# The second MoE's first layer as seven block products per unit, with the tokens in two rounds

## The chip, the core and the metric

The kernel runs on one core of a Trainium2 chip. The metric is the device time of one execution in microseconds. Five engines matter: TensorE (PE; its weight loads are listed apart, as PEld), VectorE (DVE), ScalarE (ACT), GpSimd (POOL) and SyncE (SP), which issues all transfers here. TensorE adds up its sums in PSUM, eight banks of 512 float32 per partition; the other memory is SBUF.

## What is computed

An attention with packed queries, then two MoE layers on 2304 tokens of 512 features. The change is in the last one.

```python
def _moe_ref(x, w_in, w_out):                  # first MoE: 512 -> 2048 -> 512
    h = np.maximum(x @ w_in, 0.0)
    return (h * h @ w_out)

def _moe2_ref(x, w_gate, w1, w2):              # second MoE: 8 experts, 512 -> 1024 -> 512
    P = np.exp(logits - logits.max())          # logits = x @ w_gate
    for _ in range(8):                         # the balance
        P /= P.sum(1, keepdims=True) + 1e-09
        P /= P.sum(0, keepdims=True) + 1e-09
        P *= N / E
    for e in range(E):
        h = np.maximum(x @ w1[e], 0.0)
        out += P[:, e:e + 1] * (h @ w2[e])     # every expert on every token
```

## The kernel before

Values are kept to float32 precision by splitting: a number is the sum of a rounded high half and the rest, both of the type float32r, and a product is three matmuls: high x high, high x low, low x high (a loop over `(x, y)` in `(0, 0), (0, 1), (1, 0)`). ScalarE writes the high half, VectorE (for activations) or GpSimd (for weights) subtracts it for the low half.

The stages follow one another: attention of four batches, the first MoE (`g_unit`, `h1_unit` and `x2_unit`; chunks of 288 tokens, result transposed in `X2`), the gate (`logits`, `gate_exp`, then eight steps of `rows_step` and `cols_step`), the second MoE. A scheduler sets the order of each engine's instructions from the order in which they are written; all queues run in order.

In the second MoE the 8 x 1024 hidden features are 16 groups `g` of 512, each of four columns `m` of 128. The tokens are five chunks, four of 512 and one of 256. `split_x` has split the whole of `X2` into `XS` before. `h2_mm` (L512) forms the hidden features of a chunk and one `m`: four blocks of 128 input features x three matmuls into one bank, 12 matmuls. `h2_evac` reads it out: ScalarE writes the high half with its ReLU (L520), VectorE the low half (L521). `y_unit` (L536) forms 128 tokens of the output: four `m` x three matmuls, 12 again, with the hidden features stationary and w2 moving. VectorE adds it, times the gate's column, to `acc` in SBUF (L549; L546 for the first expert, whose factors come late). A group's weights are loaded once, 2 x 2 transfers of 512 KB (L90), and are split by `split_w` (L120 on ScalarE, L121 on GpSimd) during the group before.

Four PSUM banks serve `h2_mm` and four `y_unit`. `logits` is a split product as well, with the gate's weights padded to 128 columns (L460), and is turned round by 18 transposes (L465); the balance takes its column sums with a float32 matmul of all ones (`cols_mm`, L492).

## Time and profile before

| | us |
|---|---|
| median of three runs | 2027.56 (2023.48 to 2029.18) |
| the profiled execution, its own time | 2027.71 |
| its span, first to last instruction | 2025.9 |
| TensorE busy | 1998.5 |
| VectorE / ScalarE / GpSimd busy | 771.9 / 502.5 / 261.5 |
| first layer of the second MoE on TensorE (L512) | 804.4 |
| second layer (L536) | 798.4 |
| first MoE on TensorE (L332, L313) | 234.7, 128.5 |

Busy times of matmuls count from start to a modelled end, and neighbours overlap; what a matmul costs is read from the distance of the work that they release.

### The profile page before, as it was taken

How to read it: one execution, taken by the hardware profiler on the slowest of the kernel's cores; microseconds unless marked ns; L12 is line 12 of the kernel's file. 1: busy time of each engine (PE TensorE's matmuls, PEld its weight loads, DVE VectorE, ACT ScalarE, POOL GpSimd, SP SyncE). 2: the span in 40 equal slices, each digit the busy share in tenths (PEclk: the TensorE clock that was granted, in tenths of full speed). 3: DMA queues.
4: the chain of work that ended last, by engine and by line, in shares of the span. 5: the costliest groups of instructions: out<-in, count | busy, mean ns of one | idle time of the engine just before them, and what ended most of it. 6: DMA issues, size and time to landing. Idle time of an engine off the chain costs nothing.

```text
span 2025.9 us, 24381 instructions
## 1 busy us (share of the span) xinstructions
PE 1998.5 (99%) x10250; PEld 1719.0 (85%) x10250; DVE 771.9 (38%) x1376; ACT 502.5 (25%) x987; POOL 261.5 (13%) x209
## 2 busy tenths in 40 slices
PE   8999999999999999999999999999999999999999
PEld 6898999998888888888888888888888888888887
DVE  5979887654222222222222222222222222222222
ACT  3646454532323121202021211111112121111110
POOL 2313321210202020202020202010101010110100
PEclk8999999999999999999999999999999999999999
DMA  7402210100001010101010101010000000000011
GB/s 254 157 22 75 72 43 22 43 22 1 32 11 43 1 42 0 42 1 42 1 42 0 42 1 42 1 42 11 32 11 32 11 32 11 31 14 29 1 42 52
DMA packets 21549, 71.04 MB, mean 35 GB/s; under 512 B 2368, under 2 KB 2368, under 8 KB 21440
## 3 DMA queue, kind: packets, MB, share of 16 engines
q1 hardware_dynamic: 21440, 69.49, 10.0%
q8 instruction: 80, 1.31, 0.3%
...
## 4 chain that ended last, share of the span: by engine, by line
PE 91%; DVE 7%; issue 1%; ACT 1%; POOL 0%; DVEq 0%; POOLq 0%; ACTq 0%
PE psh L512 39%; PE psy L536 39%; PE psy L332 7%; PE psh L313 3%; PE pp L200 1%; DVE cc L101 1%; DVE h L322 1%; DVE cm L105 1%; DVE g L300 1%; DVE s L320 1%; DVE cx L107 1%; PE psh L290 1%; PE s L168 0%; DVE x L339 0%; PE s L230 0%
## 5 line engine op out<-in xcount | busy, mean ns | idle before, releaser
L512 PE MATMUL psh<-x,w 128*128 128x512 f32 (+1 forms) x3840 | 804.4, 368 | 0.0
L536 PE MATMUL psy<-w,hh 128*128 128x512 f32 x3456 | 798.4, 389 | 0.0
L512 PEld LDWEIGHTS psh<-x,w 128*128 128x128 f32 x3840 | 670.4, 188 | 121.0
L536 PEld LDWEIGHTS psy<-w,hh 128*128 128x128 f32 x3456 | 647.4, 188 | 133.6
L520 ACT ACTIVATE hh<-psh 128x512 fp32r<-128x512 f32 (+1 forms) x320 | 177.6, 555 | 1203.0 <-PE psh L512 1202.9
L521 DVE SCALAR_TENSOR_TENSOR hh<-psh,hh 128x512 fp32r<-128x512 f32 (+1 forms) x320 | 204.0, 637 | 611.7 <-ACT hh L520 611.7
L549 DVE SCALAR_TENSOR_TENSOR acc<-psy,P,acc 128x512 f32<-128x512 f32 x252 | 189.1, 751 | 464.5 <-PE psy L536 464.5
L121 POOL TENSOR_TENSOR w<-raw,w 128x512 fp32r<-128x512 f32 x128 | 165.5, 1309 | 1424.4 <-ACT w L120 1413.0
L332 PE MATMUL psy<-h,w 128*128 128x288 f32 x1536 | 234.7, 297 | 7.6 <-DVE h L322 4.6
L332 PEld LDWEIGHTS psy<-h,w 128*128 128x128 f32 x1536 | 213.6, 188 | 12.4 <-DVE h L322 7.0
L313 PE MATMUL psh<-at,g 128*128 128x288 f32 x768 | 128.5, 296 | 2.3 <-DVE s L320 2.3
L313 PEld LDWEIGHTS psh<-at,g 128*128 128x128 f32 x768 | 111.0, 188 | 4.1 <-DVE s L320 3.2
L120 ACT ACTIVATE w<-raw 128x512 fp32r<-128x512 f32 x128 | 79.5, 626 | 43.3 <-PE psy L536 37.0
L321 ACT ACTIVATE h<-s 128x288 fp32r<-128x288 f32 x128 | 56.6, 443 | 74.5 <-DVE s L320 68.8
L322 DVE TENSOR_TENSOR h<-s,h 128x288 fp32r<-128x288 f32 x128 | 69.8, 549 | 8.5 <-ACT h L321 6.9
L320 DVE SCALAR_TENSOR_TENSOR s<-psh,r 128x288 f32<-128x288 f32 x128 | 57.4, 450 | 31.8 <-ACT r L317 31.2
L121 POOL TENSOR_TENSOR w<-cx,w 128x512 fp32r<-128x512 f32 x32 | 45.0, 1407 | 161.3 <-ACT w L120 125.9
L317 ACT ACTIVATE r<-psh 128x288 f32<-128x288 f32 x128 | 51.4, 404 | 49.3 <-PE psh L313 48.6
L103 POOL TENSOR_TENSOR cc<-cc,cr 128x512 int32<-128x512 int32 x32 | 45.3, 1417 | 46.7 <-DVE cc L101 30.1
L339 DVE TENSOR_TENSOR x<-psy,x 128x288 f32<-128x288 f32 x96 | 42.8, 451 | 20.9 <-PE psy L332 20.7
L300 DVE TENSOR_TENSOR g<-psh,g 64x512 fp32r<-64x512 f32 x64 | 43.6, 686 | 5.6 <-ACT g L299 4.4
L299 ACT ACTIVATE g<-psh 64x512 fp32r<-64x512 f32 x64 | 37.4, 591 | 11.0 <-PE psh L290 6.7
...
## 6 DMA issues: line engine op xcount, KB each, us to landing
raw<-w SPq DMA_DIRECT2D x64, 512.0 KB, 3.4
raw<-win SPq DMA_DIRECT2D x16, 512.0 KB, 3.8
raw<-wout SPq DMA_DIRECT2D x16, 512.0 KB, 3.8
...
```

The source lines that it names most:

```text
L120: nc.scalar.activation(w[:, 0, :], t, AF.Copy)
L121: nc.gpsimd.tensor_tensor(w[:, 1, :], t, w[:, 0, :].bitcast(F32), op=ALU.subtract)
L300: nc.vector.tensor_tensor(lo, ps[r:r + 64, :], hi.bitcast(F32), op=ALU.subtract)
L313: nc.tensor.matmul(ps, gw[:, x, m * 128:(m + 1) * 128], at[:, y, g, o:o + CT], start=(i == 0), stop=(i == 5))
L320: nc.vector.scalar_tensor_tensor(s, ps, 0.0, r, op0=ALU.max, op1=ALU.mult)
L322: nc.vector.tensor_tensor(h[:, 1, :], s, h[:, 0, :].bitcast(F32), op=ALU.subtract)
L332: nc.tensor.matmul(ps, w[:, x, d * 128:(d + 1) * 128], h[:, y, :], start=(i == 0), stop=(i == 11))
L512: nc.tensor.matmul(ps[:, :n], w[:, x, kd * 128:(kd + 1) * 128], XS[c][:, y, kd, :], start=(i == 0), stop=(i == 11))
L520: nc.scalar.activation(h[:, 0, :n], ps[:, :n], AF.Relu)
L521: nc.vector.scalar_tensor_tensor(h[:, 1, :n], ps[:, :n], 0.0, h[:, 0, :n].bitcast(F32), op0=ALU.max, op1=ALU.subtract)
L536: nc.tensor.matmul(ps, h[:, x, t * 128:(t + 1) * 128], w[:, y, :], start=(i == 0), stop=(i == 11))
L549: nc.vector.scalar_tensor_tensor(a, ps, P[:, tt, e:e + 1], a, op0=ALU.mult, op1=ALU.add)
```

## The change

The first layer of the second MoE is computed by the Strassen scheme with seven products. For a half-group of 256 hidden features the weights (512 inputs x 256 outputs) are four blocks of 256 inputs x 128 outputs: `A11`, `A12` belong to the first 128 outputs, `A21`, `A22` to the second. A group of tokens is cut into two halves, and its inputs are four blocks `B11`, `B12`, `B21`, `B22` (first index: inputs, second: half of the tokens). With S1 = A21 + A22, S2 = S1 - A11, S3 = A11 - A21, S4 = A12 - S2 and T1 = B12 - B11, T2 = B22 - T1, T3 = B22 - B12, T4 = B21 - T2, the four blocks of the result come out of A11 B11, A12 B21, S1 T1, S2 T2, S3 T3, S4 B22 and A22 T4. Each product is 2 x 3 matmuls, 42 a unit where 48 stood.

`unit` writes this out with three banks. X takes A11 B11, then S2 T2, S3 T3 and A22 T4 are added on top of what stands in it; between them X is copied to `s12` by ScalarE, and added to `s5` by VectorE. Y takes A12 B21, Z takes S1 T1 and S4 B22. Three additions on VectorE (L634, L645, L648) and three copies on ScalarE (L632, L639, L641) a unit are new, two of the additions in PSUM.

- Tokens: three groups `GROUPS` of 768, 512 and 1024, so products have 384, 256 and 512 columns. Round one runs groups 0 and 1 through the 32 half-groups of weights, round two runs group 2 through them in reverse; the half-group at the turn serves both. So weights are loaded 63 times a half-group, 126 transfers of 512 KB.
- `w1_blocks` forms S1 to S4 with four GpSimd operations of 256 columns per half-group; the splits of w1 are then four (the last of half width) instead of two for the same weights.
- `split_x` and `x_sums` split seven blocks per token group (B11, B21, B22, T1 to T4) at the start of group and round.
- `y_unit` sums two `m` instead of four: six matmuls (L596) and one accumulation on VectorE (L614), 576 of them instead of 288. They have two banks (`ybank`) instead of four; X, Y and Z of two units have six.
- `logits` is now 72 float32 matmuls (L513) with the tokens stationary and the gate's 8 columns moving; the transposes go. `X2` is held by token groups, so the additions of two chunks of the first MoE are in two pieces.

```diff
+NQ = 2 * NG
 NT = T // 128
-CHUNKS = [(c * 512, min(512, T - c * 512)) for c in range(-(-T // 512))]
+GROUPS = [(0, 384), (768, 256), (1280, 512)]
+ROUNDS = ((0, 1), (2,))
...
-    for g in range(NG):
-        for nm, src in (("w1", w1), ("w2", w2)):
-            for i in (0, 2):
-                splits += [((nm, g, i), len(loads), 0), ((nm, g, i + 1), len(loads), 1)]
-                loads.append(("f32", src[g, :, i:i + 2, :]))
+    seq2 = list(range(NQ)) + list(range(NQ - 2, -1, -1))
+    for n, g in enumerate(seq2):
+        for nm, src, parts in (("w1", w1, 4), ("w2", w2, 2)):
+            splits += [((nm, n, i), len(loads), i) for i in range(parts)]
+            loads.append(("f32", src[g // 2, :, 2 * (g % 2):2 * (g % 2) + 2, :].rearrange("p m n -> p (m n)")))
...
+    def w1_blocks(r, i):
+        a11, a12, a21, a22 = (r[:, j * 256:(j + 1) * 256] for j in range(4))
+        if i == 0:
+            t = wpools[2].tile([128, 1024], F32, tag="wt", name="wt", bufs=1)
+            s1, s2, s3, s4 = (t[:, j * 256:(j + 1) * 256] for j in range(4))
+            nc.gpsimd.tensor_tensor(s1, a21, a22, op=ALU.add)
+            nc.gpsimd.tensor_tensor(s2, s1, a11, op=ALU.subtract)
+            nc.gpsimd.tensor_tensor(s3, a11, a21, op=ALU.subtract)
+            nc.gpsimd.tensor_tensor(s4, a12, s2, op=ALU.subtract)
+            sums["t"] = t
+        return (r[:, 0:512], sums["t"][:, 0:512], sums["t"][:, 512:1024], a22)[i]
...
+            elif key[0] == "w2":
+                t = raw[l][:, i * 512:(i + 1) * 512]
+            else:
+                t = w1_blocks(raw[l], i)
+            n = t.shape[1]
             part = k % 12 >= 8
             w = wpools[part].tile([128, 2, 512], F32R, tag="w", name="w", bufs=4 if part else 8)
-            nc.scalar.activation(w[:, 0, :], t, AF.Copy)
-            nc.gpsimd.tensor_tensor(w[:, 1, :], t, w[:, 0, :].bitcast(F32), op=ALU.subtract)
+            nc.scalar.activation(w[:, 0, :n], t, AF.Copy)
+            nc.gpsimd.tensor_tensor(w[:, 1, :n], t, w[:, 0, :n].bitcast(F32), op=ALU.subtract)
...
-    X2 = [xpa.tile([128, 4, CT], F32, tag="xa", name="x2", bufs=4) for _ in range(4)]
+    X2 = [xpa.tile([128, 4, 2 * n], F32, tag=f"xa{p}", name=f"x2_{p}") for p, (_, n) in enumerate(GROUPS[:2])]
+    def x2_parts(c):
+        for p, (t0, n) in enumerate(GROUPS):
+            u, w = max(t0, c * CT), min(t0 + 2 * n, (c + 1) * CT)
+            if u < w:
+                yield p, slice(u - t0, w - t0), slice(u - c * CT, w - c * CT)
...
-        o = X2[c][:, d, :]
-        if f == 0:
-            nc.scalar.activation(o, ps, AF.Copy)
-        else:
-            nc.vector.tensor_tensor(o, ps, o, op=ALU.add)
...
+        for p, there, here in x2_parts(c):
+            o = X2[p][:, d, there]
+            if f == 0:
+                nc.scalar.activation(o, ps[:, here], AF.Copy)
+            else:
+                nc.vector.tensor_tensor(o, ps[:, here], o, op=ALU.add)
+    XC = {}
+    def split_x(p, name, src, where, engine):
+        n = GROUPS[p][1]
+        t = where.tile([128, 2, 2, n], F32R, tag=f"xc{p}", name=f"xc{p}", bufs=XCB[p, where])
+        nc.scalar.activation(t[:, 0], src, AF.Copy)
+        engine.tensor_tensor(t[:, 1], src, t[:, 0].bitcast(F32), op=ALU.subtract)
+        XC[p, name] = t
+    def x_block(p, i, j):
+        n = GROUPS[p][1]
+        return X2[p][:, 2 * i:2 * i + 2, j * n:(j + 1) * n]
+    def x_sums(p, where, temps, engine):
+        n = GROUPS[p][1]
+        t1 = temps.tile([128, 2, n], F32, tag="s12", name="t1", bufs=2)
+        nc.vector.tensor_tensor(t1, x_block(p, 0, 1), x_block(p, 0, 0), op=ALU.subtract)
+        split_x(p, "T1", t1, where, engine)
+        nc.vector.tensor_tensor(t1, x_block(p, 1, 1), t1, op=ALU.subtract)
+        split_x(p, "T2", t1, where, engine)
+        t3 = temps.tile([128, 2, n], F32, tag="s12", name="t3", bufs=2)
+        nc.vector.tensor_tensor(t3, x_block(p, 1, 1), x_block(p, 0, 1), op=ALU.subtract)
+        split_x(p, "T3", t3, where, engine)
+        nc.vector.tensor_tensor(t1, x_block(p, 1, 0), t1, op=ALU.subtract)
+        split_x(p, "T4", t1, where, engine)
...
+            stXA, xca = open_pool("xca", side="left")
+            XCB[0, xca] = 3
+            for name, i, j in (("B11", 0, 0), ("B21", 1, 0), ("B22", 1, 1)):
+                split_x(0, name, x_block(0, i, j), xca, nc.gpsimd)
...
+    stPS2.close()
+    stPSB.close()
+    psm = pool("psm", space=PSUM)
...
+    def ybank():
+        return psm.tile([128, 512], F32, tag="y", name="psy", bufs=2)
...
+        psk = ybank()[:, :NT * E].rearrange("p (t e) -> p t e", t=NT)
+        for p, (t0, n) in enumerate(GROUPS):
+            for t in range(2 * n // 128):
+                for kd in range(4):
+                    nc.tensor.matmul(psk[:, t0 // 128 + t, :], X2[p][:, kd, t * 128:(t + 1) * 128], wgr[:, kd, :],
+                                     start=(kd == 0), stop=(kd == 3))
+        return psk
...
+    def balance():
+        if steps["n"] < 0 or steps["n"] >= 8:
+            return
+        cols_step(steps["cs"])
...
+    def product(ps, n, p, a, b, start):
+        i, o = WHERE[a]
+        w, x = W["w1", n, i], XC[p, b]
+        N = GROUPS[p][1]
+        last = None
+        for k in range(2):
+            for u, v in ((0, 0), (0, 1), (1, 0)):
+                nc.tensor.matmul(ps[:, :N], w[:, u, o + k * 128:o + (k + 1) * 128], x[:, v, k, :],
+                                 start=(start and k + u + v == 0), stop=(k == 1 and u == 1), skip_group_check=True)
+    def evac(key, src, p):
+        N = GROUPS[p][1]
+        h = hp.tile([128, 2, N], F32R, tag="hh", name="hh", bufs=HB[p])
+        nc.scalar.activation(h[:, 0, :], src, AF.Relu)
+        nc.vector.scalar_tensor_tensor(h[:, 1, :], src, 0.0, h[:, 0, :].bitcast(F32), op0=ALU.max, op1=ALU.subtract)
+        H2[key] = h
...
+        for t in [*range(per, 2 * per), *range(per)]:
+            yield lambda t=t: y_unit(n, p, t // per, t % per, t)
...
+        ps = ybank()
+        i = 0
+        for m in range(2):
+            w = W["w2", n, m]
+            h = H2[n, p, m, half]
+            for x, y in ((0, 0), (0, 1), (1, 0)):
+                nc.tensor.matmul(ps, h[:, x, o * 128:(o + 1) * 128], w[:, y, :], start=(i == 0), stop=(i == 5))
+                i += 1
...
+        if n == first:
+            if p < 2:
+                nc.scalar.activation(a, ps, AF.Copy)
+            else:
+                nc.scalar.activation(a, ps, AF.Copy, scale=P[:, tt, e:e + 1])
+        elif p < 2 and e == 0:
+            nc.vector.tensor_tensor(a, ps, a, op=ALU.add)
+            if g == 3:
+                nc.scalar.activation(a, a, AF.Copy, scale=P[:, tt, 0:1])
+        else:
+            nc.vector.scalar_tensor_tensor(a, ps, P[:, tt, e:e + 1], a, op0=ALU.mult, op1=ALU.add)
+        if n == late:
+            nc.sync.dma_start(out[tt * 128:(tt + 1) * 128, :], a)
...
+        X, Y, Z = (psm.tile([128, 512], F32, tag="c", name="psc", bufs=6) for _ in range(3))
+        s12 = temps.tile([128, 2, N], F32, tag="s12", name="s12", bufs=2)
+        s5 = temps.tile([128, N], F32, tag="s5", name="s5", bufs=2)
+        product(X, n, p, "A11", "B11", True)
+        nc.scalar.activation(s12[:, 0, :], X[:, :N], AF.Copy)
+        product(Y, n, p, "A12", "B21", True)
+        nc.vector.tensor_tensor(Y[:, :N], Y[:, :N], s12[:, 0, :], op=ALU.add)
+        evac((n, p, 0, 0), Y[:, :N], p)
+        after.get(0, lambda: None)()
+        y()
+        product(Z, n, p, "S1", "T1", True)
+        nc.scalar.activation(s5, Z[:, :N], AF.Copy)
+        product(X, n, p, "S2", "T2", False)
+        nc.scalar.activation(s12[:, 1, :], X[:, :N], AF.Copy)
+        after.get(1, lambda: None)()
+        y(2)
+        product(Z, n, p, "S4", "B22", False)
+        nc.vector.tensor_tensor(Z[:, :N], Z[:, :N], s12[:, 1, :], op=ALU.add)
+        evac((n, p, 0, 1), Z[:, :N], p)
+        product(X, n, p, "S3", "T3", False)
+        nc.vector.tensor_tensor(s5, X[:, :N], s5, op=ALU.add)
+        evac((n, p, 1, 1), s5, p)
+        after.get(2, lambda: None)()
+        y(2)
+        product(X, n, p, "A22", "T4", False)
+        evac((n, p, 1, 0), X[:, :N], p)
+        after.get(3, lambda: None)()
+        y(len(ys))
...
+    def group1():
+        gate_exp(gate["psk"])
+        steps["n"], steps["cs"] = 0, rows_step()
+        for name, i, j in (("B11", 0, 0), ("B21", 1, 0), ("B22", 1, 1)):
+            split_x(1, name, x_block(1, i, j), xcb, nc.gpsimd)
+        x_sums(1, xcb, xcb, nc.vector)
...
+    last = None
+    for n in range(NQ):
+        for p in ROUNDS[0]:
+            if n == 0 and p == 0:
+                after = {0: start_gate, 1: lambda: split_w(2), 3: group1}
+            else:
+                k = 2 if p == 0 else 1
+                after = {i: (lambda i=i: (split_w(k if i < 2 else 0), balance())) for i in range(4)}
+            unit(n, p, xcb, y_units(*last) if last else (), after)
+            last = n, p
+    for y in y_units(*last):
+        y()
+    stH.close()
+    stXB.close()
+    stXA.close()
+    stXC, xcc = open_pool("xcc", side="left")
+    hp = pool("hp2", side="right")
+    XCB[2, xcc] = 7
+    split_x(2, "B11", x_block(2, 0, 0), xcc, nc.vector)
+    split_x(2, "B21", x_block(2, 1, 0), xcc, nc.gpsimd)
+    x_sums(2, xcc, xcc, nc.vector)
+    split_x(2, "B22", x_block(2, 1, 1), xcc, nc.gpsimd)
+    last = None
+    for n in range(NQ - 1, 2 * NQ - 1):
+        after = {0: lambda: split_w(1), 1: lambda: split_w(2), 2: lambda: split_w(1)}
+        unit(n, 2, xcc, y_units(*last) if last else (), after)
+        split_w(2)
+        last = n, 2
```

What the scheduler makes of it is shown at three places.

TensorE in the steady second MoE of before (`psh` are the banks of the first layer, `x_...` the token chunks, `psy` those of y):

```order
L512 MATMUL psh<-x_4791,w 128x512 x24
L512 MATMUL psh<-x_5238,w 128x512 x24
L536 MATMUL psy<-w,hh 128x512 x48
L512 MATMUL psh<-x_5238,w 128x512 x24
L512 MATMUL psh<-x_5245,w 128x512 x24
L536 MATMUL psy<-w,hh 128x512 x48
```

TensorE in one unit of round two of after (`xc_13119` is B11, 13122 B21, 13127 T1, 13131 T2, 13136 T3, 13143 B22, 13140 T4; six matmuls on `psy` are one y unit, of an earlier half-group):

```order
L568 MATMUL psc<-xc_13119,w 128x512 x6
L568 MATMUL psc<-xc_13122,w 128x512 x5
L596 MATMUL psy<-w,hh 128x512 x6
L568 MATMUL psc<-xc_13122,w 128x512
L596 MATMUL psy<-w,hh 128x512 x6
L568 MATMUL psc<-xc_13131,w 128x512 x6
L596 MATMUL psy<-w,hh 128x512 x12
L568 MATMUL psc<-xc_13136,w 128x512 x6
L568 MATMUL psc<-xc_13127,w 128x512 x6
L596 MATMUL psy<-w,hh 128x512 x12
L568 MATMUL psc<-xc_13143,w 128x512 x6
L568 MATMUL psc<-xc_13140,w 128x512 x6
```

Blocks of 24 and 48 have become pieces of 6 and 12, and between two products on one bank (B11, T2, T3, T4) there stand y units or products on another.

VectorE in a steady group of before:

```order
L549 SCALAR_TENSOR_TENSOR acc<-psy,P,acc 128x512 x4
L521 SCALAR_TENSOR_TENSOR hh<-psh,hh 128x512 x2
L521 SCALAR_TENSOR_TENSOR hh<-psh,hh 128x256 x2
L549 SCALAR_TENSOR_TENSOR acc<-psy,P,acc 128x512 x4
L521 SCALAR_TENSOR_TENSOR hh<-psh,hh 128x256 x2
```

VectorE in one unit of round two of after (`s_16518` is the unit's `s12`, `s_16519` its `s5`, `s_16207` the `s5` of two units before):

```order
L634 TENSOR_TENSOR psc<-psc,s_16518 128x512
L614 SCALAR_TENSOR_TENSOR acc_13275<-psy,P,acc_13275 128x512
L575 SCALAR_TENSOR_TENSOR hh<-s_16207,hh 128x512
L575 SCALAR_TENSOR_TENSOR hh<-psc,hh 128x512
L614 SCALAR_TENSOR_TENSOR acc_13275<-psy,P,acc_13275 128x512 x2
L648 TENSOR_TENSOR s_16519<-psc,s_16519 128x512
L614 SCALAR_TENSOR_TENSOR acc_13275<-psy,P,acc_13275 128x512 x2
L575 SCALAR_TENSOR_TENSOR hh<-psc,hh 128x512
L645 TENSOR_TENSOR psc<-psc,s_16518 128x512
L575 SCALAR_TENSOR_TENSOR hh<-psc,hh 128x512
L614 SCALAR_TENSOR_TENSOR acc_13275<-psy,P,acc_13275 128x512 x3
```

Seven operations that follow products stand between eight accumulations, and the low halves of the hidden features come one to two units after their products.

TensorE at the gate of after (`x_0`, `x_1`, `x_2` are the token groups in `X2`, `xc_4814` and 4817 B11 and B21 of group 0, 5280 and 5284 its T1 and T2, 5456 and on the blocks of group 1):

```order
L568 MATMUL psc<-xc_4814,w 128x384 x6
L568 MATMUL psc<-xc_4817,w 128x384 x6
L513 MATMUL psy<-wgr,x_0_104 128x8 x24
L513 MATMUL psy<-wgr,x_1_105 128x8 x16
L513 MATMUL psy<-wgr,x_2_1340 128x8 x32
L568 MATMUL psc<-xc_5280,w 128x384 x6
L568 MATMUL psc<-xc_5284,w 128x384 x6
L568 MATMUL psc<-xc_5456,w 128x256 x6
```

In before the gate's matmuls (L460, 40 of them, and 18 transposes L465) stand in pieces between matmuls of L332, L512 and L536; now they are one block between the second and the third product.

## Rows read from the trace of the kernel before

**Rows 1.** Page of the profile, part 1; span and mean granted clock of the core.

```profile
PE 1998.5 (99%) x10250; PEld 1719.0 (85%) x10250; DVE 771.9 (38%) x1376; ACT 502.5 (25%) x987; POOL 261.5 (13%) x209
...
core 0: 2025.9 us, clock 0.997
```

**Rows 2.** Groups by form, whole span: instruction xcount | busy us, mean ns | idle before.

```profile
L536 PE MATMUL psy<-w,hh 128*128 128x512 f32 x3456 | 798.4, 389 | 0.0
L512 PE MATMUL psh<-x,w 128*128 128x512 f32 x3072 | 712.3, 389 | 0.0
L512 PEld LDWEIGHTS psh<-x,w 128*128 128x128 f32 x3840 | 670.4, 188 | 121.0
L549 DVE SCALAR_TENSOR_TENSOR acc<-psy,P,acc 128x512 f32<-128x512 f32 x252 | 189.1, 751 | 464.5 <-PE psy L536 464.5
L521 DVE SCALAR_TENSOR_TENSOR hh<-psh,hh 128x512 fp32r<-128x512 f32 x256 | 176.8, 691 | 543.9 <-ACT hh L520 543.9
L121 POOL TENSOR_TENSOR w<-raw,w 128x512 fp32r<-128x512 f32 x128 | 165.5, 1309 | 1424.4 <-ACT w L120 1413.0 <-issue 7.3
L520 ACT ACTIVATE hh<-psh 128x512 fp32r<-128x512 f32 x256 | 153.1, 598 | 1010.0 <-PE psh L512 1009.8
L120 ACT ACTIVATE w<-raw 128x512 fp32r<-128x512 f32 x128 | 79.5, 626 | 43.3 <-PE psy L536 37.0 <-PE psy L332 3.5 <-DMA raw<-w 0.8
L521 DVE SCALAR_TENSOR_TENSOR hh<-psh,hh 128x256 fp32r<-128x256 f32 x64 | 27.1, 424 | 67.9 <-ACT hh L520 67.9
L546 DVE TENSOR_TENSOR acc<-psy,acc 128x512 f32<-128x512 f32 x18 | 12.4, 691 | 33.6 <-PE psy L536 33.6
```

**Rows 3.** Timeline, second MoE: start us, duration us, engine, line, operation, xcount.

```profile
659.30 0.60 ACT L520 ACTIVATE hh<-psh 128x512 fp32r<-128x512 f32 x1 [2.12 <-PE psh L512]
661.76 6.51 PE L536 MATMUL psy<-w,hh 128*128 128x512 f32 x28
662.02 0.60 ACT L520 ACTIVATE hh<-psh 128x512 fp32r<-128x512 f32 x1 [2.12 <-PE psh L512]
664.68 0.75 DVE L549 SCALAR_TENSOR_TENSOR acc<-psy,P,acc 128x512 f32<-128x512 f32 x1 [1.34 <-PE psy L536]
667.40 0.75 DVE L549 SCALAR_TENSOR_TENSOR acc<-psy,P,acc 128x512 f32<-128x512 f32 x1 [1.97 <-PE psy L536]
...
2000.87 0.38 ACT L520 ACTIVATE hh<-psh 128x256 fp32r<-128x256 f32 x1 [0.84 <-PE psh L512]
2002.31 0.38 ACT L520 ACTIVATE hh<-psh 128x256 fp32r<-128x256 f32 x1 [1.06 <-PE psh L512]
```

**Rows 4.** Timeline: float32 matmuls of the attention, and the gate.

```profile
54.61 4.68 PEld L230 LDWEIGHTS s<-bd,qt 128*128 128x128 f32 x40
...
454.48 0.54 PE L465 MATMUL psh<-ident,lgT 16*128 16x16 f32 x6
455.05 0.46 DVE L471 COPY lg<-psh 128x288 f32<-128x288 f32 x1 [1.22 <-PE psh L465]
459.88 0.43 DVE L487 TENSOR_REDUCE cs<-P 128x8 f32<-128x144 f32 x1
...
464.61 0.28 PE L492 MATMUL psh<-cs,ones 128*128 128x8 f32 x2
```

**Rows 5.** Timeline: first and last work of the second MoE.

```profile
434.38 2.61 PEld L512 LDWEIGHTS psh<-x,w 128*128 128x128 f32 x12
...
2021.33 1.41 DVE L549 SCALAR_TENSOR_TENSOR acc<-psy,P,acc 128x512 f32<-128x512 f32 x2 [4.40 <-PE psy L536]
```

**Rows 6.** Busy time in a stretch of the first MoE, then granted clock, DMA share, GB/s.

```profile
200.00:300.00 100.00, 97.27 (x703) 94.64 (x702) 86.26 (x170) 53.11 (x114) 28.20 (x21) 1.00 0.17 54
```

**Rows 7.** Page, part 6 (issue to landing, us), and the timeline at 435 us.

```profile
raw<-w SPq DMA_DIRECT2D x64, 512.0 KB, 3.4
...
435.50 2.87 POOL L121 TENSOR_TENSOR w<-raw,w 128x512 fp32r<-128x512 f32 x1 [59.53 <-ACT w L120]
435.87 1.35 DVE L349 TENSOR_TENSOR x<-x,x 128x1152 fp32r<-128x1152 f32 x1
```

More of the change, by code (lines that the diff above doesn't have):

```diff
@@ new lines, with start_gate @@
+    XCB[0, xcb] = 4
+    XCB[1, xcb] = 7
+    x_sums(0, xcb, xcb, nc.vector)
+    gate = {}
+    def group1():
[4 more added lines that the diff above has]
+        x_sums(1, xcb, xcb, nc.vector)
+    def start_gate():
+        gate["psk"] = logits()
+    last = None
[8 more added lines that the diff above has]
+            last = n, p
@@ L594 @@
+    for y in y_units(*last):
+        y()
+    stXC.close()
 def kernel(**inputs):
```

171 lines of the change are left out of this document (43 added, 128 removed).

## The prediction

> **What bounds the kernel now.** I read the page's busy times first: TensorE is busy for 1998.5 of 2025.9 us, at a granted clock of 0.997, so at the 2.4 GHz level; VectorE stands at 38%, ScalarE at 25%, GpSimd at 13% [rows 1]. A busy TensorE need not be TensorE at its peak, so the second view is the timeline of the second MoE, to find what one matmul costs there. Two evictions of 12-matmul sums start at 659.30 and 662.02, and two accumulations of y at 664.68 and 667.40: 12 matmuls of 512 columns in 2.72 us, 226.7 ns each. The two sums of 256 columns at the end are read 1.44 us apart: 120.0 ns each [rows 3]. Both lie on one line, 13.3 ns + columns / 2.4 GHz; a 384-column matmul, which the trace lacks, comes to 173.3 ns by it. With that, one of the 16 weight groups costs 4 x 48 x 0.2267 + 48 x 0.120 = 49.3 us in the first layer and 18 x 12 x 0.2267 = 49.0 us in the second, and 16 groups cost 788.5 + 783.5 = 1572.0 us. From the first weight load of the first layer (434.38) to the last accumulation (2021.33) the trace has 1587.0 us [rows 5]. So 15 us hold everything that is no product, the gate with it: TensorE's instruction stream is the bound, and no wait in this stage is worth hunting. The third view, the groups by form, says the same: no idle time before any matmul of the two layers, while VectorE and ScalarE wait for it [rows 2].
>
> **The products (the term that carries the sum).** Removed are 3840 matmuls, 788.5 us. Added are 96 units (32 half-groups of weights by three token groups) of 7 x 6 = 42 matmuls, of which a third each has 384, 256 and 512 columns: 1344 x (0.1733 + 0.120 + 0.2267) = 698.9 us. That is **-89.6 us**, a bit less than the eighth (98.6) that the arithmetic promises, since 192 more instructions each pay the 13.3 ns and shorter ones pay it on fewer columns. The second layer keeps its 3456 matmuls of 512 columns; only its sums are half as deep.
>
> Weights load behind the matmuls: a weight load shows 188 ns [rows 2], longer than the 120 ns in which a 256-column matmul follows the next, so loads overlap and set no floor at 256 columns. The Trainium skill, "TensorE: Matmul & The Clock Gate", Part 3 (The mechanism), says that a weight load overlaps a running matmul only when it targets other row groups. By that, each full-array matmul here would pay its load on top; what this would give is the fourth rival below.
>
> **The evictions.** They multiply, off TensorE. In round two (512 columns) a unit now costs VectorE 8 accumulations at 0.751, four low halves and three additions at 0.691 (the additions are nearest to the accumulation of that form, PSUM plus SBUF) [rows 2]: 10.8 us of the unit's 90 x 0.2267 = 20.4 us. In round one a pair of units takes VectorE 10 x 0.751 + 7 x 0.42 + 7 x 0.56 (between the 256 and 512 forms) = 14.4 of 25.9 us. ScalarE: 7 x 0.598 + 5 x 0.626 + 0.4 = 7.7 of 20.4. GpSimd: five subtractions of 1.31, one of half that width and four block sums of half that width (0.65 each, in proportion) = 9.8 of 20.4. No engine but TensorE is over 56%. On the path they cost what TensorE waits for.
>
> So I followed one unit of round two through the order shown above, with the rows' durations. A sum is read 0.26 us after its last matmul gives way to the next (661.76, 662.02) [rows 3]. T2's sum must be copied before T3 adds to its bank: 0.26 + 0.60 = 0.86 us, and two y units, 2.72 us, lie between: 1.9 spare. T4 needs the sum with T1's copy: T1 ends 1.36 after T3, its copy 0.86 later, the addition 0.69 later, 2.9 us after T3's end, and T1, two y units and B22 fill 5.4: 2.5 spare. A y unit needs its bank back, of which there are two now instead of four: 0.26 + 0.75 = 1.01 us. Where pairs of y stand apart by a product there are 2.72 us for it, 1.7 spare, which two waiting 0.69 operations of VectorE just fit into. I take 4 us for all 96 units (bounds 0 and, if each unit loses half of a 0.69 operation, 34).
>
> **The gate.** The split product with padded weights goes (32 x 0.2267 + 8 x 0.120 = 8.2 us), with 18 transposes at (0.54 - 0.213) / 5 = 0.065, 1.2 us [rows 4]. In its place stand 72 float32 matmuls with 8 moving columns, and the trace shows each float32 matmul as two records (20 of L230 as 40). Nearest is the balance's own matmul: float32, 8 columns, two records 0.067 apart (0.28 less one of 0.213). 144 x 0.067 = 9.7; bounds 0.065, and 0.115 as L230's 128 columns run (4.68 us for 40) [rows 4]: 9.4 to 16.6. **+0.3 us** (0 to +7). Behind it, the chain from the copy of the logits to the first column sums took 455.05 to 460.31, 5.3 us [rows 4]; in the new order TensorE has 4.9 us of products in front of the first balance matmul, and VectorE comes late to the chain, since the blocks of the next token group stand ahead of it: **+3** (0 to +8).
>
> **The rest.** In the first MoE the additions into X2 of two chunks of eight fall into two pieces: 24 more operations on VectorE, of 128 and 160 columns and so under the 0.42 of 256 [rows 2]. TensorE is at 97% there and VectorE at 86% [rows 6]: **+1** (0 to +6). At the turn to round two VectorE forms four differences and five low halves of 1024 elements, 1.2 us each in proportion to 1.35 for 1152 [rows 7], 10.8 us, among six accumulations, 4.5; TensorE has six y units and three products of two units by then, 16.4 us: **+2** (0 to +6). The weights come twice, 126 transfers of 512 KB instead of 64. Cover: 3.4 us from issue to landing [rows 7], two transfers per 20 us or more. The last accumulation and transfer end as before.
>
> **Sum.** Against the profiled execution's own 2027.71 (0.15 above the median of 2027.56, so nothing is shifted): -89.6 + 0.3 + 3 + 1 + 2 + 4 = -79.3, so **1948 us**. With every wait at zero it is 1938, and the runs of before scatter by 4 downwards: 1934.
>
> **Rivals.** First, the y banks: VectorE waits inside its own queue for ScalarE or for TensorE, the accumulation behind it comes late and two banks don't cover it. For: VectorE's load doubles and TensorE's banks for y halve. Against: 1.7 us spare where I followed it. At 0.35 per unit, 96 x 0.35 = 34: 1982 us. Second, the weights: in every other unit of round two ScalarE's order has the copy of a freshly loaded piece ahead of the copies of the block sums that the next T2 needs; if the transfer is late by its whole landing, 16 x 3.4 = 54: 2002 us. GpSimd can stretch too: one subtraction took 2.87 us instead of 1.31 beside a VectorE operation with both inputs in SBUF [rows 7]. The Trainium skill, "GPSIMD Engine Reference", section 8, names just this contention; the row agrees.
>
> Third, slower than before: the chain in a unit is exposed. Four products pass through one bank and are read between. The links are 0.26 + 0.60, the same again, and 0.26 + 0.69: 2.67 us at 512 columns, with the 256 forms (0.38 and 0.42 [rows 2, 3]) 1.96, between them 2.3: 32 x 6.95 = 222 us, 2170 in all. From 79 / 222 = 36% of it on, the change loses. Against it: the other unit and the y units stand between the links in the order. Fourth, loads that don't overlap: 0.188 more for each matmul, so the products would go from 1510 to 1457 and the time to 2027.7 - 54 + 10 = 1984. The 1587.0 us of the stage [rows 5] leave no room for 3840 + 3456 loads of 0.188. That the seven products aren't there is excluded by the order (4032 matmuls).
>
> **How the numbers follow.** Forecast 0.78 (1934 to 1962), y banks 0.12, weights 0.05, chain 0.04, loads 0.01. All but the chain end faster by more than 0.3%, which is about what a measurement of this kernel tells from no change; with a little of the second rival's tail: faster 0.95, same 0.01, slower 0.04. The range 1934 to 1982 holds the forecast and most of the first rival and leaves out some 0.16.
>
> **What would show it.** In the profile after: 384- and 256-column products 173 and 120 ns apart; a pair of units in round one every 25.9 us and a unit in round two every 20.4; TensorE's idle time before products and y units of a few us in all, most at the gate and the turn. Wrong would be: idle time before L596 released by VectorE (first rival), before L568 by GpSimd or ScalarE (second, third). A granted clock below 1.00 after the gate's small matmuls, which fill few columns, would be another; no row prices it.

## The result, and the profile after the change

The changed kernel takes **1969.9 us** (median of four runs, 1968.4 to 1973.3) against 2027.6 us before: a ratio of 0.972 (95% interval 0.970 to 0.974), 57.7 us less. The prediction said 1948 us, 79.6 less, with 1934 to 1982 around it. The sign and the mechanism were right; 22 us of the expected gain did not come, and the result lies above 1962, where the forecast's own part of the range ended. The profiled execution of the changed kernel took 1970.19 us, 57.5 less than that of before.

First the page of the profile after (busy times; granted clock in 40 slices of the span of 1968.4 us), which answers [rows 1].

```profile
PE 1937.2 (98%) x10528; PEld 1718.6 (87%) x10528; DVE 1156.9 (59%) x2046; ACT 772.6 (39%) x1597; POOL 754.3 (38%) x718
PEclk8999999997999999999999999999999999999999
```

TensorE is still the bound, at 98%, though VectorE went from 38% to 59%. New is the 7 in the tenth slice of the clock: near 440 to 490 us TensorE ran well below its 2.4 GHz for a part of the time. The groups by form answer [rows 2] (instructions xcount | busy us, mean ns of one | idle time before them and what ended it).

```profile
L596 PE MATMUL psy<-w,hh 128*128 128x512 f32 x3456 | 870.1, 392 | 1.3 <-DVE acc L614 1.3
L568 PE MATMUL psc<-xc,w 128*128 128x512 f32 x1344 | 336.1, 391 | 1.6 <-ACT xc L380 1.5
L568 PE MATMUL psc<-xc,w 128*128 128x384 f32 x1344 | 265.9, 338 | 0.0
L568 PE MATMUL psc<-xc,w 128*128 128x256 f32 x1344 | 196.7, 281 | 1.6 <-DVE hh L575 1.6
...
L513 PE MATMUL psy<-wgr,x 128*128 128x8 f32 x144 | 27.4, 337 | 0.0
```

The 4032 products are there, a third in each size, and before them and the y units TensorE waits 4.5 us in all for other engines (1.3 + 1.6 + 1.6). So the missing 22 us are not waits. One row stands out: the gate (L513), 144 records, 27.4 us. The forecast had 9.7.

The timeline at the gate (start us, duration us, engine, line, operation, xcount; it also answers [rows 5] with the first weight load of the stage):

```profile
433.97 2.05 PEld L568 LDWEIGHTS psc<-xc,w 128*128 128x128 f32 x12
...
436.18 27.45 PE L513 MATMUL psy<-wgr,x 128*128 128x8 f32 x144
463.48 6.82 PE L568 MATMUL psc<-xc,w 128*128 128x384 f32 x33
```

And the stretches of it (busy time and instructions of PE, PEld, DVE, ACT, POOL; then the granted clock, DMA share, GB/s):

```profile
436.20:439.00 2.80, 2.80 (x28) 2.80 (x26) 2.73 (x2) 1.24 (x2) 2.80 (x3) 1.00 0.47 167
440.00:463.00 23.00, 23.00 (x109) 23.00 (x110) 11.76 (x12) 4.55 (x7) 10.84 (x8) 0.50 0.07 24
463.50:467.00 3.50, 3.50 (x12) 3.50 (x13) 2.13 (x8) 0.91 (x2) 0.38 (x1) 0.50 0.00 0
...
1294.00:1305.00 11.00, 8.22 (x23) 5.85 (x24) 9.78 (x9) 2.34 (x3) 3.04 (x1) 0.69 0.35 121
```

From 436.2 to 439 the clock is 1.00 and 28 matmuls are counted in 2.8 us, two or three of them cut by its borders: 0.11 us each. From 440 on it is 0.50, the 1.2 GHz level, and a record takes 23 / 109 = 0.21 us. TensorE has no idle time there; what it did since 436 were the gate's 8-column matmuls and nothing else. The products behind it run at 0.50 too, until 467.

ScalarE's copy of a unit's first product (L632) shows the period of the two rounds:

```profile
889.75 0.49 ACT L632 ACTIVATE s<-psc 128x384 f32<-128x384 f32 x1 [1.48 <-PE psc L568]
...
942.10 0.49 ACT L632 ACTIVATE s<-psc 128x384 f32<-128x384 f32 x1 [1.42 <-PE psc L568]
...
1649.52 0.60 ACT L632 ACTIVATE s<-psc 128x512 f32<-128x512 f32 x1 [5.36 <-PE psc L568]
...
1690.32 0.60 ACT L632 ACTIVATE s<-psc 128x512 f32<-128x512 f32 x1 [5.36 <-PE psc L568]
```

In round one 52.35 us lie between equal places of the order, which repeats after two pairs of units: 26.18 a pair, where 25.92 was forecast. In round two 40.80 for two units: 20.40 each, exactly the forecast. The turn between the rounds, and the last accumulation of the kernel:

```profile
1293.47 0.98 PE L568 MATMUL psc<-xc,w 128*128 128x512 f32 x2
1295.95 1.60 PE L568 MATMUL psc<-xc,w 128*128 128x512 f32 x4 [1.50 <-ACT xc L380]
1298.83 2.93 PE L596 MATMUL psy<-w,hh 128*128 128x512 f32 x6 [1.28 <-DVE acc L614]
...
1964.61 0.75 DVE L614 SCALAR_TENSOR_TENSOR acc<-psy,P,acc 128x512 f32<-128x512 f32 x1 [0.61 <-PE psy L596]
```

Two short waits, and the clock is 0.69 from 1294 to 1305.

**The account.** The stage runs from 433.97 to 1964.61, 1530.6 us. The products at the forecast's prices are 698.9 + 783.5 = 1482.4, so 48.2 us are left for everything else; before it was 15.0, and the forecast's terms made 24.3 of it. To place the 48.2, I counted in each stretch the matmuls that start there, at the prices of the line of [rows 3], and took the sum from the stretch's length.

| Part of the stage | forecast, us | after, us |
|---|---|---|
| the gate's matmuls | 9.7 | 27.3 |
| start behind the gate, and the old rest of before | 3 + 5.6 | 4.7 + 2.2 |
| round and unit losses (520 to 1293, 1340 on) | 4 | 7.6 + 0.1 |
| turn to round two | 2 | 6.3 |

That is 23.9 us more than forecast inside the stage; the first MoE ended 0.4 earlier where 1 later was forecast, and the tail is 0.8 shorter: -79.3 + 23.9 - 1.4 - 0.8 = -57.6, against -57.5 measured.

### The profile page after: what moved, and what is told of

Read it like the earlier page. It is cut to its first block, busy times and chain, and to the rows that moved or that the text cites. A ratio compares the mean times of both kernels' runs of the same rounds, so it can differ in the third digit from the quotient of the medians.

```text
span 1968.4 us, 27132 instructions
## 1 busy us (share of the span) xinstructions
PE 1937.2 (98%) x10528; PEld 1718.6 (87%) x10528; DVE 1156.9 (59%) x2046; ACT 772.6 (39%) x1597; POOL 754.3 (38%) x718
## 3 DMA queue, kind: packets, MB, share of 16 engines
q1 hardware_dynamic: 30368, 102.00, 15.3%
## 4 chain that ended last, share of the span: by engine, by line
PE 89%; DVE 8%; DMA 1%; issue 1%; ACT 1%; POOL 0%; SPq 0%; DVEq 0%; ACTq 0%
PE psy L596 40%; PE psc L568 35%; PE psy L364 7%; PE psh L345 3%; PE psy L513 1%; PE pp L225 1%; DVE cc L105 1%; DVE h L354 1%; DVE cm L109 1%; DVE g L325 1%; DVE s L352 1%; DVE cx L111 1%; DMA raw<-win 1%; PE psh L315 1%; DVE x L372 1%
## 5 line engine op out<-in xcount | busy, mean ns | idle before, releaser
L596 PE MATMUL psy<-w,hh 128*128 128x512 f32 x3456 | 870.1, 392 | 1.3 <-DVE acc L614 1.3
L568 PE MATMUL psc<-xc,w 128*128 128x256 f32 (+2 forms) x4032 | 780.3, 337 | 3.2 <-DVE hh L575 1.6
L568 PEld LDWEIGHTS psc<-xc,w 128*128 128x128 f32 x4032 | 676.2, 189 | 81.1 <-ACT xc L380 2.3
L596 PEld LDWEIGHTS psy<-w,hh 128*128 128x128 f32 x3456 | 636.3, 188 | 120.4 <-DVE acc L614 3.2
L614 DVE SCALAR_TENSOR_TENSOR acc<-psy,P,acc 128x512 f32<-128x512 f32 x528 | 395.0, 748 | 404.5 <-PE psy L596 403.1
L146 POOL TENSOR_TENSOR w<-raw,w 128x512 fp32r<-128x512 f32 (+1 forms) x252 | 301.5, 1202 | 467.8 <-ACT w L145 456.2
L146 POOL TENSOR_TENSOR w<-wt,w 128x512 fp32r<-128x512 f32 x126 | 162.8, 1299 | 366.9 <-ACT w L145 366.9
L145 ACT ACTIVATE w<-raw 128x512 fp32r<-128x512 f32 (+1 forms) x252 | 143.0, 573 | 324.8 <-PE psc L568 172.7
L575 DVE SCALAR_TENSOR_TENSOR hh<-psc,hh 128x256 fp32r<-128x256 f32 (+2 forms) x288 | 156.3, 548 | 64.4 <-ACT hh L574 64.4
L574 ACT ACTIVATE hh<-psc 128x256 fp32r<-128x256 f32 (+2 forms) x288 | 139.5, 487 | 89.4 <-PE psy L596 84.5
L632 ACT ACTIVATE s<-psc 128x384 f32<-128x384 f32 (+1 forms) x96 | 46.9, 489 | 188.5 <-PE psc L568 185.1
L145 ACT ACTIVATE w<-wt 128x512 fp32r<-128x512 f32 x126 | 79.1, 628 | 94.3 <-PE psc L568 62.9
L648 DVE TENSOR_TENSOR s<-psc,s 128x384 f32<-128x384 f32 (+1 forms) x96 | 53.4, 556 | 80.7 <-ACT s L639 56.7
L634 DVE TENSOR_TENSOR psc<-psc,s 128x384 f32<-128x384 f32 (+1 forms) x96 | 53.6, 560 | 62.7 <-PE psc L568 33.0
L639 ACT ACTIVATE s<-psc 128x384 f32<-128x384 f32 (+1 forms) x96 | 46.7, 487 | 88.5 <-PE psc L568 86.9
```

Of the source, the lines that this page charges most:

```text
L145: nc.scalar.activation(w[:, 0, :n], t, AF.Copy)
L146: nc.gpsimd.tensor_tensor(w[:, 1, :n], t, w[:, 0, :n].bitcast(F32), op=ALU.subtract)
L568: nc.tensor.matmul(ps[:, :N], w[:, u, o + k * 128:o + (k + 1) * 128], x[:, v, k, :], start=(start and k + u + v == 0), stop=(k == 1 and u ...
L574: nc.scalar.activation(h[:, 0, :], src, AF.Relu)
L575: nc.vector.scalar_tensor_tensor(h[:, 1, :], src, 0.0, h[:, 0, :].bitcast(F32), op0=ALU.max, op1=ALU.subtract)
L596: nc.tensor.matmul(ps, h[:, x, o * 128:(o + 1) * 128], w[:, y, :], start=(i == 0), stop=(i == 5))
```

## The experiments

The leading theory for the gate (the **clock theory**): a run of nearly empty matmuls brings the granted clock down to half, and that makes the block 27 us. Its rival (the **load theory**): a float32 weight load costs that much at any clock. All ratios below are to the kernel before, measured beside each run; the changed kernel stands at 0.9721 on that scale. One thing blurs comparisons of totals: in the profiled executions of the changed kernel and its variants the first product of the second MoE, behind a first MoE whose code is the same in all, started between 430.7 and 436.0 us. So sizes are taken from stretches, and totals only confirm them.

**Matmuls by themselves (e1_bench).** A kernel of matmuls alone, in the order that the expectation lists.

> Matmuls alone, nothing else of the computation: 240 of 512, 384 and 256 columns each with a new stationary block; then four times the mix that one n of round one has (42 of 384, 42 of 256, 60 of 512 columns in sixes); then, each between stretches of 512 columns, the gate's 72 float32 matmuls as one block with 8, with 128 and with 64 moving columns, as nine pieces of 8 with 24 of 512 columns between, and 144 fp32r matmuls of 8 columns. Clock theory (TensorE's clock falls in a run of nearly empty matmuls, and that doubles their time): the 8-column block takes about 27 us, its first 3 us at 0.085 us a record and clock 1.00, the rest at 0.19 and 0.50; the 128-column block stays at 1.00 and takes 144 x 0.115 = 16.6 us; the pieces stay at 1.00, 9 x 16 x 0.085 = 12.2 us in all; the fp32r block falls to 0.50 as well. Load theory (a float32 weight load costs 0.19 us whatever the clock): 8, 64 and 128 columns take 27 us each, and so do the pieces in sum. Mix: 4 x 25.92 = 103.7 us if 384 columns cost 173.3 ns, as the forecast has it; 4 x 26.18 = 104.7 if round one's extra time is of TensorE alone.

Its timeline (L71 are the 512, L76 the 384, L81 the 256 columns; L86, L92, L98 the gate's matmuls with 8, 128, 64 columns; L124 the fp32r ones):

```profile
62.71 41.79 PE L76 MATMUL psa<-mv,st 128*128 128x384 f32 x240
104.33 28.95 PE L81 MATMUL psb<-mv,st 128*128 128x256 f32 x240
133.12 1.55 PE L71 MATMUL psx<-mv,st 128*128 128x512 f32 x6
134.51 1.23 PE L76 MATMUL psa<-mv,st 128*128 128x384 f32 x6
...
239.62 13.79 PE L71 MATMUL psx<-mv,st 128*128 128x512 f32 x60
253.25 27.40 PE L86 MATMUL psg<-wgr,xf 128*128 128x8 f32 x144
...
309.56 16.24 PE L92 MATMUL psg<-wide,xf 128*128 128x128 f32 x144
...
352.85 1.85 PE L86 MATMUL psg<-wgr,xf 128*128 128x8 f32 x16
...
432.03 16.18 PE L98 MATMUL psg<-wide,xf 128*128 128x64 f32 x144
...
475.35 27.61 PE L124 MATMUL psg<-mv,st 128*128 128x8 f32 x144
```

And its stretches, with the granted clock third from the end (the first row counts the matmuls of L86 alone):

```profile
253.60:256.60 3.00, 3.00 (x29) 1.00 0.00 0
...
257.00:280.00 23.00, 23.00 (x109) 23.00 (x109) 0.00 (x0) 0.00 (x0) 0.00 (x0) 0.50 0.00 1
...
309.60:325.50 15.90, 15.90 (x144) 15.90 (x143) 0.00 (x0) 0.00 (x0) 0.00 (x0) 1.00 0.00 1
353.00:412.00 59.00, 59.00 (x330) 51.04 (x328) 0.00 (x0) 0.00 (x0) 0.00 (x0) 1.00 0.00 1
...
480.00:502.00 22.00, 22.00 (x105) 22.00 (x105) 0.00 (x0) 0.00 (x0) 0.00 (x0) 0.50 0.00 1
```

The 8-column block takes 27.4 us with nothing else on the chip's engines, and runs at 0.50 from 257 on, as in the kernel. With 64 or with 128 columns, eight and sixteen times the work, it takes 16.2 us at a clock of 1.00. The fp32r block, which holds no float32 matmul, falls too. That is the clock theory; the load theory is out as the cause of the 27 us. But it has a share: in pieces between other matmuls the clock stays at 1.00, and a piece still takes 1.70 us (from 352.85 to the next block). Inside a piece, and in the block before its clock falls, the records start 0.111 us apart (29 in the first row's 3.00 us, two of them cut by its borders); only the first two of a block start 0.026 apart. With 64 and with 128 columns they start 0.111 apart too, and so do those of the fp32r block at first. So at full clock a record costs that with 8, 64 or 128 columns, float32 or fp32r, and 144 are 16.0 us, not the 12.2 of the expectation, nor the 9.7 of the forecast. That it is the weight load which sets this price is not shown. Of the 27.3 us, then, 6.3 above the forecast are the record's own price and 11.3 the clock.

The sizes: 384 columns cost (104.33 - 62.71) / 240 = 173.4 ns, so the interpolated 173.3 was right. The mix of round one takes (239.62 - 134.51) / 4 = 26.28 us where its parts add to 25.92: round one's loss is TensorE's own, and no other engine is needed for it. What in the mix costs it is for e5_bench2.

**No gate (e2_gate_none).**

```
-        nc.vector.tensor_copy(P, psk)
+        nc.vector.memset(P, 0.0)
...
-        gate["psk"] = logits()
+        pass
```

> The gate's 72 matmuls are left out and its logits are set to 0; all else stays. Both theories: at most 27.3 us less than the changed kernel, and a few more for the half-clock products behind the block, 1940 at the least. What it tells is how much of the block lies beside work that TensorE would have waited for anyway: the sums and splits of group 0's blocks ran on VectorE from 434.7 to 449.2. If they were free, 1940 to 1943; if TensorE now waits for them, up to 9 us more, 1952.

1950.9 us, 0.9628 (0.9612 to 0.9644): 19 us less, not 27. The waits of TensorE from 434 to 460 tell why (us in total, times, longest):

```profile
PE psc L568 <- ACT s L632: 3.2, 1, 3.2
PE psc L568 <- POOL xc L381: 2.8, 1, 2.8
PE psc L568 <- ACT xc L380: 1.2, 1, 1.2
```

Without the block TensorE waits over 7 us for group 0's sums and splits (L380, L381), and the copies behind them; the lower clock that follows (0.52 from 450 to 460) comes on top. The block had covered that work. The profiled execution was the slowest of the four, 1955.8 us at a mean clock of 0.991 against 1949.6 to 1951.0 at 0.994 to 0.996, and its stage is 15.3 us shorter than the changed kernel's (1515.4 against 1530.6). So the gate's matmuls are worth 15 to 19 us in place, and their cover must be kept when they are made faster.

**The gate padded (e3_gate_wide).**

```
-    wgr = gc.tile([128, 4, E], F32, name="wgr")
-    nc.sync.dma_start(wgr, wg)
+    wgr = gc.tile([128, 4, 128], F32, name="wgr")
+    nc.gpsimd.memset(wgr, 0.0)
+    nc.sync.dma_start(wgr[:, :, 0:E], wg)
...
-                    nc.tensor.matmul(psk[:, t0 // 128 + t, :], X2[p][:, kd, t * 128:(t + 1) * 128], wgr[:, kd, :],
+                    o = E * (t0 // 128 + t)
+                    nc.tensor.matmul(ps[:, o:o + 128], X2[p][:, kd, t * 128:(t + 1) * 128], wgr[:, kd, :],
```

> The gate's weights padded with zeros from 8 to 128 moving columns; same 72 matmuls, same place, 16 times the columns. Clock theory: clock stays at 1.00, 144 records x 0.115 = 16.6 us in place of 27.3, and no half-clock products behind: 1970 - 10.7 - 0 to 2 = 1957 to 1960. Load theory: 27 us or more, 1970 or above.

1973.1 us, 0.9729 (0.9715 to 0.9744): no gain, against the clock theory's 1957 to 1960. Yet the block did what that theory says. The timeline, first at the gate, then in round two:

```profile
438.07 16.24 PE L515 MATMUL psy<-wgr,x 128*128 128x128 f32 x144
...
1516.87 1.56 PE L598 MATMUL psy<-w,hh 128*128 128x512 f32 x6
1518.27 1.53 PE L570 MATMUL psc<-xc,w 128*128 128x512 f32 x6
1519.64 1.56 PE L598 MATMUL psy<-w,hh 128*128 128x512 f32 x6
```

The block is 11 us shorter, and the stretch behind it runs at 1.00. What it won goes for the most part in round two, 850 us later (11.8 us there, 2.3 in round one): a y unit takes 1.40 us there and a product 1.37, where the changed kernel has 1.36 for both. Nothing waits, and the clock is 1.00. What the edit moved is the memory: its larger gate tile pushes the h tiles 1920 bytes down, from a byte address of 128 to one of 0 modulo 256 in each partition, while w2 stays at 128. That gave a new theory, the **address theory**, which e5 to e7 test.

**The gate in pieces (e4_gate_spread).** `logits` makes two token tiles at a time and copies each piece to P at once.

```
-                after = {0: start_gate, 1: lambda: split_w(2), 3: group1}
+                after = {0: logits, 1: lambda: (split_w(2), logits()), 2: logits, 3: group1}
...
-                after = {i: (lambda i=i: (split_w(k if i < 2 else 0), balance())) for i in range(4)}
+                after = {i: (lambda i=i: (split_w(k if i < 2 else 0), logits() if tiles else balance())) for i in range(4)}
```

> The same 72 matmuls of 8 columns in nine pieces of two token tiles, between the products of the first three units. Clock theory: clock 1.00, 144 x 0.085 = 12.2 us in place of 27.3, so -15, and up to +9 where TensorE now waits for the sums of group 0 that the block covered: 1953 to 1964. Load theory: 27 us in all, and the same wait: 1970 to 1979.

1973.9 us, 0.9735 (0.9719 to 0.9751): inside the load theory's range and 10 us over the clock theory's. By the total the load theory wins; the waits of TensorE from 436 to 530 and a stretch show that the total misleads:

```profile
PE psy L545 <- DVE cs L540: 3.4, 1, 3.4
PE psc L575 <- ACT s L639: 2.7, 1, 2.7
```

```profile
445.00:465.00 20.00, 17.44 (x76) 16.93 (x77) 13.98 (x22) 8.51 (x18) 7.80 (x7) 0.66 0.08 27
```

As without the gate, the cover is gone: TensorE waits 2.7 us for a copy that stands behind the splits of the sums on ScalarE (L639), its clock falls to a mean of 0.66 for 20 us, and the balance waits 3.4 us for VectorE. Whether these waits or the 8-column pieces lowered the clock, this run does not separate. A later piece, at full clock, took 1.71 us for its 16 records, as in e1_bench.

**Addresses and sizes by themselves (e5_bench2).**

> Matmuls alone again, with stationary and moving operands placed at byte addresses of 0 or of 128 modulo 256 in a partition (the changed kernel has 128 for all of them, the kernel with the padded gate 0 for the stationary h and 128 for the moving w2). Address theory: 512 columns take 226.7 ns with both at 128, about 232.5 with the stationary at 0 and the moving operand at 128, and 227.3 with both at 0, as in the first series. Then round one's mix of 42 of 384, 42 of 256 and 60 of 512 columns, all at 128, in blocks of six, in blocks of twelve, and in three long runs. Switch theory (a change of size from block to block costs some 13 ns): 26.2, 26.05 and 25.92 us a mix. If the mix of the first series was slow from its addresses alone: 25.92 for all three.

Four stretches of 512 columns (stationary/moving at 128/128, 128/0, 0/128, 0/0), then 432 matmuls, three mixes each, in sixes, in sixes with the 512-column blocks at 0/128, in long runs and in twelves. A count takes in one to three matmuls that were still running when the stretch began, and the last two stretches of 512 columns begin two matmuls early:

```profile
29.75:55.83 26.07, 26.07 (x116) 1.00 0.00 1
65.61:83.81 18.20, 18.20 (x79) 1.00 0.00 0
91.73:109.70 17.97, 17.97 (x78) 1.00 0.00 0
119.73:141.75 22.01, 22.01 (x98) 1.00 0.00 0
...
209.87:288.71 78.84, 78.84 (x434) 1.00 0.00 1
288.71:367.41 78.70, 78.70 (x435) 1.00 0.00 1
367.41:445.29 77.88, 77.88 (x435) 1.00 0.00 1
445.29:523.93 78.64, 78.64 (x435) 1.00 0.00 1
```

26.07 / 115 = 226.7 ns with both operands at 128, 18.20 / 78 = 233.3 and 17.97 / 77 = 233.4 where one is at 128 and the other at 0 (either way round), 22.01 / 97 = 226.9 with both at 0. So it is not the address itself but the difference of the two that costs 3%. Apart from multiples of 512 bytes, only differences of 0 and 128 were tried; whether one of 256 costs anything is not shown. At the end of the run, blocks of six at 128/128 and at 0/128 by turns take 1.37 and 1.40 us, as the product and the y unit do in round two of e3_gate_wide.

The mixes: 78.84 / 3 = 26.28 us in sixes, 25.96 in long runs, 26.21 in twelves. The switch theory holds: matmuls of one size follow each other at the line's price, and changes of size cost 0.3 us in a mix of 24 blocks. Twelves recover less than expected. And one set goes against the address theory as it stood: in sixes with the 512-column blocks at 0/128 a mix takes 78.70 / 3 = 26.23 us, no more than at 128/128, where 60 matmuls at 6.7 ns would add 0.4. The difference of the addresses costs where 512-column matmuls follow each other, as in round two, and not in a mix of sizes.

**The padded gate with the addresses put right (e6_wide_al)**, and **the addresses alone put wrong (e7_shift)**. Both edits are one line, the second in the changed kernel itself:

```
-    gc.tile([128, 24], F32, name="gpad")
+    gc.tile([128, 56], F32, name="gpad")
```

> The padded gate again, with 128 bytes of filler more, so that the h tiles lie at 128 modulo 256 bytes as in the changed kernel. Address theory: round two's matmuls are back at 226.7 ns, 12 us less than with the padded gate alone: 1958 to 1961, which is 9 to 12 us under the changed kernel, the block's saving. If it is the padded gate itself that slows round two: 1973 as before.

> The changed kernel with 128 bytes of filler more and nothing else: the h tiles move from 128 to 0 modulo 256 bytes. Address theory: 1536 matmuls of y in round two at 232.9 and 1344 of the products at 229.1 ns in place of 226.7, 12.7 us more: 1980 to 1984. If addresses do nothing: 1970.

1954.8 us, 0.9644 (0.9624 to 0.9663), and 1986.8, 0.9796 (0.9778 to 0.9814). The same 500 us of round two in the changed kernel, in e6_wide_al and in e7_shift, in this order (e3_gate_wide has 2166 matmuls there, as e7_shift):

```profile
1400.00:1900.00 500.00, 500.00 (x2207) 414.30 (x2206) 262.53 (x368) 173.01 (x317) 245.12 (x242) 1.00 0.15 51
```

```profile
1400.00:1900.00 500.00, 500.00 (x2208) 414.01 (x2207) 263.03 (x368) 174.23 (x320) 249.53 (x247) 1.00 0.17 53
```

```profile
1400.00:1900.00 500.00, 500.00 (x2166) 407.08 (x2165) 258.26 (x361) 171.66 (x312) 243.07 (x240) 1.00 0.16 51
```

2207 matmuls or 2166 in the same time, by 128 bytes of filler. For round two the address theory holds in both directions. e7_shift lost 17 us where 12.7 was expected: round two lost 12 (41 matmuls, 9.3 us, in these 500 us alone), and the rest came in round one (2.5), at its start (1.7) and at the turn (1.1), which the expectation had left out. The y units of round one had moved as well, and at 6.7 ns each their 1920 matmuls would have lost 12.8 us; that they lost 2.5 at the most fits the mixes of e5_bench2. e6_wide_al has its gate block in 433.97 to 449.97, 16.0 us. Of its 15 us, 11.3 are the block, 1 the start and turn, and 2.2 an earlier end of the first MoE, which is not the edit's.

**Group 2's blocks ahead of the turn (e8_turn).** Its block halves go into the buffers that groups 0 and 1 leave.

```
+    early2 = {0: lambda: block2("B11", 0, 0, nc.gpsimd), 1: lambda: block2("B21", 1, 0, nc.gpsimd), 2: sum_t1, 3: lambda: sum_t2(0)}
...
+            if n == NQ - 1 and p == 1:
+                after = {i: (lambda i=i: (split_w(k if i < 2 else 0), early2[i]())) for i in range(4)}
...
+    rest2()
     for y in y_units(*last):
         y()
```

> Group 2's blocks are kept in halves in the buffers that groups 0 and 1 leave, so that seven of the fourteen halves are ready before the turn to round two. Theory of the late blocks (TensorE waited 3.3 us at the turn for blocks and accumulations, and ran some 10 us at a clock of 0.65 behind that): of 8.6 us at the turn 1 to 4 are left, 1962 to 1966. Rival (VectorE has the same sums to make, and they are late anyway): 1968 to 1971.

1968.3 us, 0.9706 (0.9689 to 0.9723): within the interval of the changed kernel. Its waits at the turn:

```profile
PE psy L597 <- DVE acc L615: 2.7, 2, 2.3
PE psy L597 <- ACT hh L575: 1.2, 1, 1.2
```

The waits for blocks are gone, and the clock is 1.00 from 1274 to 1305. But VectorE, busy for 8.96 of the 9 us from 1274 on, makes the same sums, now among the accumulations of y, and these come late: 3.9 us of waits in place of 2.8. By the count of matmuls the turn costs 1.5 us less. So each theory had a part: the half clock was a cost, and VectorE is the bound at the turn.

**An eighth product (e9_eighth).**

```
         product(X, n, p, "A11", "B11", True)
+        product(X, n, p, "A11", "B11", True)
```

> The product A11 x B11 is made twice in every unit (the second overwrites the first), so eight products stand where seven stood. If the seven cost what the forecast took, one more costs 32 x 6 x (0.1733 + 0.120 + 0.2267) = 99.8 us: 2069.7. If TensorE in truth had spare time in a unit (waits hidden by other engines' work), less than 95: under 2065. Eight would then cost 798.7 us in all, against 788.5 before the change in chunks of 512 columns.

2068.2 us, 1.020 (1.018 to 1.022): 98 us more. A product costs TensorE what the forecast paid for it; units have no slack in which one hides.

**Both gains (e10_best1, e11_best2).** e10 is e6_wide_al with e8_turn; e11 moves two operations in it to GpSimd, and in the last unit of round one puts the block work ahead of the weight splits:

```
-        half("T2", k, t, nc.vector)
+        half("T2", k, t, nc.gpsimd)
...
-            half("T3", k, t3[:, k, :], nc.vector)
+            half("T3", k, t3[:, k, :], nc.gpsimd)
...
-                after = {i: (lambda i=i: (split_w(k if i < 2 else 0), early2[i]())) for i in range(4)}
+                after = {i: (lambda i=i: (early2[i](), split_w(k if i < 2 else 0))) for i in range(4)}
```

> Padded gate with the h tiles at 128 modulo 256 bytes, and group 2's blocks in halves ahead of the turn. If the two gains add: 1954.8 - 2 to -5 = 1950 to 1953. If the turn was late only because of what the gate left behind: 1955.

> As the one before, with the low halves of T2 and T3 of group 2 on GpSimd and its block work ahead of the weight splits. At the turn TensorE had waited 2.3 us for an accumulation that stood on VectorE behind these sums. If VectorE is the bound there: 1 to 3 us less, 1948 to 1951. If GpSimd is too slow for it (1.3 to 1.7 us a half in place of 0.7), 1952 to 1955.

1956.1 us (0.9648, 0.9630 to 0.9665) and 1955.2 (0.9643, 0.9627 to 0.9659): neither can be told from e6_wide_al, and the gains of 2 to 5 and of 1 to 3 us that were hoped for do not show in the totals. By the count of matmuls the turn costs 1.4 and 2.1 us less than there, but the first MoE happened to end 3.7 us later in both profiled executions. No version is measurably better than e6_wide_al, which has the simplest edit: 1954.8 us, 15 under the changed kernel and 72 under the one before.

## Why the prediction was right, and where it fell short

**The bound and the products: right.** TensorE's stream is the bound before and after. 384 columns cost 173.4 ns where 173.3 was interpolated, round two's unit takes the forecast 20.40 us, and an eighth product costs 98 us against the forecast's 99.8. The -89.6 us came.

**The range: kept by luck.** The forecast's own part of it ended at 1962. The part above, up to 1982, was there for late y banks, and these cost one wait of 1.3 us. 1969.9 lies in that part for another reason, the gate.

**The gate: the step that failed.** The prediction put 144 records at 0.067 us, "nearest is the balance's own matmul", +0.3 us in all with +7 as the upper bound; it came to +17.9. Two errors lie in it. The two records of a balance matmul were taken as the rate of a long run of such matmuls, and their distance was misread as well: the trace of before has them 0.026 us apart (they last 0.170 and 0.256), as the first two of any block, while the 40 of L230 start 0.111 apart. At full clock a long run costs that 0.111 a record with 8 columns too (e1_bench), which only the bound from the attention's matmuls had nearly right. And both bounds came from rows at a clock of 1.00. That the clock could fall was named, with the words "no row prices it"; it fell, and cost 11.3 us. An effect that is named as unpriced belongs into the range of its term: the block at half rate, 144 x 0.23 = 33 us, could have been written down from the 0.115 alone.

**The chain behind the gate: right, by luck.** Start and old rest came to 6.9 us where 8.6 stood. But the prediction did not see that group 0's sums are late as well; the long gate block covered them (e2_gate_none).

**The steady losses: inside the bounds, wrong in kind.** 7.7 us against 4, with bounds of 0 and 34. The forecast looked for waits of TensorE on VectorE. There are almost none; the loss is the change of matmul size from block to block in round one (26.18 us a pair in the kernel, 26.28 by matmuls alone, 25.96 in long runs).

**The turn: mis-sized.** 6.3 us against 2, a little over its bound of 6. The waits were 2.8 us; the rest is the lower clock behind them (0.69 from 1294 to 1305, by estimate 0.31 x 11 = 3.4 us), which no term had.

**The rivals.** The y banks cost one wait of 1.3 us, and the weights no wait of TensorE at all. The exposed chain did not appear either. Nor did the loads: 256-column products followed each other in 120.0 ns (e1_bench), with weight loads that show a mean of 190 ns. The line of the Trainium skill, "TensorE: Matmul & The Clock Gate", Part 3 (The mechanism), by which a weight load overlaps a running matmul only on other row groups, does not describe what these runs show. The same section also lets a load into the background weight buffer go ahead of running matmuls, which would agree; that this is what happens here, no run shows.

**What stays open.** Why operands whose addresses differ by 128 bytes cost 3%, why they do not in a mix of sizes, and why a change of size costs what it does, these runs do not show; they show that it is so, and how much. That the first MoE ends up to 5 us apart was not pursued.
